# Another order of the opening's steps in a fused attention and feed-forward kernel

## The chip, the cores and the metric

The kernel runs on one core of one Trainium2 chip. The metric is the device time of one execution in microseconds (us); smaller is better.

## The reference, cut to what matters

Inputs: q, k, v of 8 batches, 8 heads, 576 tokens and 64 columns; a LayerNorm gain of 512; two weight matrices, 512 x 2048 and 2048 x 512; all float32.

```python
k_p = k.reshape(B, H, Sp, pool, D).mean(axis=3)      # pool = 8, Sp = 72
v_p = v.reshape(B, H, Sp, pool, D).mean(axis=3)
scores = scale * np.matmul(q, k_p.transpose(0, 1, 3, 2))
scores = scores - np.max(scores, axis=-1, keepdims=True)
attn = np.exp(scores)
attn = attn / (np.sum(attn, axis=-1, keepdims=True) + 1e-09)
x = np.matmul(attn, v_p)                             # heads joined: 4608 tokens x 512
xn = (x - mu) / np.sqrt(var + 1e-06) * g_ln          # over the 512 columns
out = x + np.maximum(xn @ w_ch1, 0.0) @ w_ch2
```

## The kernel before

The 4608 tokens are 36 tiles of 128, and nine chunks of four tiles. TensorE (PE) multiplies float16. Each weight and each normalized token (z) is split into a high and a low half, and a product is three matmuls (high by high, high by low, low by high).

For a token tile t, `stage_a` (A.t) loads q of tile t + 2, computes the scores (PE, L432), takes their maximum (VectorE or DVE, L441, L446), the exponentials (ScalarE or ACT, L458), splits them (ACT, and GpSimd or POOL), and sends them through a transposing DMA (L479, on SyncE's queue, SP) to give `pt`. `stage_b` (B.t) multiplies `pt` by the pooled v (PE, L537 and L538), divides by the sums (DVE, L541, L549, L551), normalizes (L562 to L632, with a chain of very short steps L619 to L621 for the inverse root), splits z (ACT L642, POOL L643) and turns it over by a transposing DMA (SP, L648). V.t is the first half of B.t, X the transposes alone.

The feed-forward part of a chunk: I.c.q is `in_quarter`, four blocks of 128 hidden columns. A block is 12 matmuls (L674) into a PSUM tile, evicted by ACT (L682) and DVE (L683) into the `ring`. O.c.h is `out_half`: for each of the chunk's four tiles 24 matmuls (L770), and one eviction on DVE (L780) that adds to x; in the second half x then goes out (SP, L784). So one O is 96 matmuls and four L780. PSUM has three tiles for these blocks, so a block can start when the third-last one before it has been evicted. The text counts the hidden blocks of chunk 0 as f0 to f15; I.0.2 holds f8 to f11, I.0.3 f12 to f15.

The kernel opens with two chunks, 0 and 1, in which it also gets the weights ready: C.m.b converts a block of matrix m, M1 and M2 take maxima for scales, S.m.b splits a block (ACT L166, DVE L171). T.h.k and U.h.k form sums of blocks of the first matrix for a product scheme of seven instead of eight partial products (DVE L277, L279, L281, POOL L278, L280; split by ACT L264 and POOL L265). HK.b.i and HV.b.i load half of a batch's k or v (SP, L299 and L312) and pool it on POOL (L304, L305, L308 for k; L318, L319, L320 for v). After a batch's last v, DVE takes its maximum (L324, then L132 and L133, with a small matmul L154) and splits it. Chunks 2 to 8 use the seven-product scheme (L705); their order is fixed by two small lists, `A_AT` and `B_AT`.

What orders the opening is the string `START`: a list of these names with their arguments. A loop calls them in that order, and so the program is recorded in that order:

```python
for token in START.split():
    name, *args = token.split(".")
    ops[name](*map(int, args))
```

The tile framework then schedules the recorded program with a timeline of its own (`schedule_with_timeline_sim=True`), so that the instructions of an engine do not stand exactly in the order of the list. Each engine runs its own instructions strictly in the order that results. After the list is through, the opening's PSUM tiles are given back, and chunks 2 to 8 follow with other PSUM pools: one for attention, and six tiles for the feed-forward part.

Of the kernel before, what the change touches and what calls it, by code (L numbers as in the profile page):

```python
# [19 lines left out]
B, H, S, D = 8, 8, 576, 64  # L20
# [34 lines left out]
Z_EXP, W1_EXP = 8, -1  # L55
OUT_EXP = -14 - W1_EXP
START = """
LD K0 A.0 C.1.0 V0 R.2.0 R.2.1 C.1.1 A.1 C.1.2 B.0 C.1.3 M1.0 S.1.0 S.1.1 S.1.2 S.1.3 R.2.2 R.2.3 B.1 A.2 I.0.0.0
A.3 B.2 I.0.1.0 LN C.2.0 B.3 C.2.1 C.2.2 C.2.3 R.1.4 R.1.5 M2.0 I.0.0.1 S.2.0 S.2.1 S.2.2 S.2.3 R.1.6 R.1.7 I.0.1.1 D.0 KN
A.4 C.1.4 C.1.5 C.1.6 VN D.1 O.0.0 C.1.7 M1.1 A.5 S.1.4 S.1.5 S.1.6 S.1.7 R.2.4 R.2.5 I.0.2 R.2.6 R.2.7 A.6 B.4 I.0.3 C.2.4 B.5 A.7 C.2.5 B.6  # L60
 C.2.6 B.7 C.2.7 M2.1  S.2.4 S.2.5 S.2.6 S.2.7 O.0.1  I.1.0 HK.2.0 HK.2.1 HV.2.0 I.1.1 HV.2.1  A.8 O.1.0
 T.1.0 T.1.1 T.0.0 T.0.1 A.9 B.8 I.1.2 HK.3.0 HK.3.1 HV.3.0 A.10 U.0.0 U.0.1 B.9 HV.3.1 A.11
V.10 I.1.3 U.1.0 U.1.1 X B.11 O.1.1
"""
RSQRT_MAGIC = float(0x5F3759DF - 0x00400000) - 2.0**31

# [841 lines left out]
```

## Time and profile before

| | before |
|---|---|
| time, median of 3 runs | 877.6 us (877.41 to 878.29) |
| time of the profiled execution | 877.42 us |
| its span in the trace | 875.7 us |
| mean granted PE clock | 0.977 |
| PE busy | 834.4 us, 95% of the span |
| DVE, ACT, POOL busy | 556.7, 324.0, 291.8 us |

The trace covers the span; the execution's own time has 1.7 us around it. Times in rows count from the span's start. A row of a timeline has start, length, engine, line, operation, output and input, the number of neighbouring instructions that it joins, and in brackets the idle time of the engine ahead of it, with what ended that. SPq is the DMA queue of SyncE. In the page's 40 slices, each digit is a busy share in tenths. The opening ends at about 279 us.

### The profile page before, as it was taken

The numbers are of one execution on the slowest core, as the hardware profiler recorded it, in microseconds if no ns is written. First come the engines' busy times: TensorE is split into PE (matmuls) and PEld (weight loads), VectorE is DVE, ScalarE is ACT, GpSimd is POOL, SyncE is SP. The second block draws the span as 40 slices with busy tenths as digits, with TensorE's granted clock in tenths as the row PEclk, the third lists the DMA queues.
The fourth block names the chain that finished last, engine by engine and source line by source line (L and its number), as shares of the span: only waits on it lengthen the run. The fifth ranks groups of instructions, "written<-read, shape, count | busy, mean of one in ns | idle before, by whom it ended". The sixth has DMA issues, their size and how long they took to land. (4 is left out here: it accounts for less than half of the span.)

```text
span 875.7 us, 14897 instructions
## 1 busy us (share of the span) xinstructions
PE 834.4 (95%) x5808; PEld 546.0 (62%) x5808; DVE 556.7 (64%) x1148; ACT 324.0 (37%) x615; POOL 291.8 (33%) x429
## 2 busy tenths in 40 slices
PE   7699896999998999999999998999999999999998
PEld 5586642454455757576767665767666676757483
DVE  4999799652376647674856486738664847494242
ACT  3797433222141524243425241524342324333140
POOL 0534687447064544245412434231111211120000
PEclk9888897999999999999999999999999999999999
DMA  9991520253154452444243415432424142322001
GB/s 354 365 385 65 127 63 7 49 134 91 37 144 122 108 113 52 121 115 120 54 124 93 98 35 137 88 76 48 126 61 71 33 115 47 51 46 64 0 1 48
DMA packets 145109, 87.35 MB, mean 100 GB/s; under 512 B 125328, under 2 KB 126480, under 8 KB 142480
## 3 DMA queue, kind: packets, MB, share of 16 engines
q1 hardware_dynamic: 143888, 85.52, 36.7%
q10 hardware_dynamic: 1152, 0.90, 0.4%
q8 instruction: 45, 0.74, 0.3%
q14 instruction: 24, 0.20, 0.1%
HBM read 45.09 MB, written 9.44 MB: 62 GB/s over the span
## 5 line engine op out<-in xcount | busy, mean ns | idle before, releaser
L770 PE MATMUL ps_f<-w,ring 128*128 128x512 f16 x1728 | 381.3, 379 | 0.0
L770 PEld LDWEIGHTS <-ring 128*128 128x128 f16 x1728 | 167.7, 98 | 193.1 <-issue 0.2
L705 PE MATMUL ps_f<-zts,w 128*128 128x256 f16 x1680 | 209.1, 274 | 7.5 <-DVE x L780 3.4
L705 PEld LDWEIGHTS <-w 128*128 128x128 f16 x1680 | 164.1, 98 | 29.7 <-issue 7.3
L780 DVE SCALAR_TENSOR_TENSOR x<-ps_f,cy,x 128x512 f32<-128x512 f32 x72 | 53.8, 748 | 120.5 <-PE ps_f L770 117.6
L674 PE MATMUL ps_f<-zts,w 128*128 128x512 f16 (+1 forms) x480 | 96.7, 363 | 10.7 <-DVE x L780 7.7
L705 PE MATMUL ps_f<-zts,tsp 128*128 128x256 f16 x672 | 96.3, 272 | 0.3 <-ACT raw L723 0.3
L746 DVE SCALAR_TENSOR_TENSOR ring<-raw,ring 128x512 f16<-128x512 f32 x112 | 83.0, 767 | 9.1 <-ACT ring L745 8.8
L469 POOL TENSOR_TENSOR phl<-e,phl 128x512 f16<-128x512 f32 x32 | 37.5, 1170 | 151.9 <-ACT phl L462 151.8
L745 ACT ACTIVATE ring<-raw 128x512 f16<-128x512 f32 x112 | 64.8, 623 | 52.4 <-DVE raw L739 52.0
L674 PEld LDWEIGHTS <-w 128*128 128x128 f16 x480 | 49.9, 105 | 51.9 <-issue 17.6
L723 ACT COPY raw<-ps_f 128x256 f32<-128x256 f32 x56 | 20.8, 372 | 140.3 <-PE ps_f L705 137.4
L705 PEld LDWEIGHTS <-tsp 128*128 128x128 f16 x672 | 64.0, 98 | 10.9 <-issue 0.7
L643 POOL TENSOR_TENSOR hl<-raw,hl 128x640 f16<-128x640 f32 x28 | 41.0, 1480 | 75.9 <-ACT hl L642 40.0
L726 DVE TENSOR_TENSOR raw<-ps_f,raw 128x256 f32<-128x256 f32 x56 | 23.7, 424 | 50.7 <-PE ps_f L705 44.6
L739 DVE TENSOR_TENSOR raw<-ps_f,raw 128x256 f32<-128x256 f32 x112 | 42.3, 418 | 21.2 <-PE ps_f L705 20.9
L318 POOL TENSOR_TENSOR vr<-vr 72x256 f32<-72x256 f32 x48 | 38.7, 813 | 47.1 <-DMA vr<-in_v_dram 46.9
L432 PE MATMUL ps_a<-kblk,q 128*128 128x144 f32 (+1 forms) x320 | 44.9, 293 | 0.0
L642 ACT CAST hl<-raw 128x640 f16<-128x640 f32 x28 | 19.2, 723 | 68.0 <-DVE raw L597 33.4
L432 PEld LDWEIGHTS ps_a<-kblk,q 128*128 128x128 f32 (+1 forms) x320 | 40.4, 183 | 5.2 <-issue 1.7
L732 DVE TENSOR_TENSOR raw<-ps_f,raw 128x256 f32<-128x256 f32 x56 | 23.6, 421 | 30.8 <-PE ps_f L705 28.0
L643 POOL TENSOR_TENSOR hl<-z,hl 128x512 f16<-128x512 f32 x18 | 21.1, 1171 | 63.0 <-ACT hl L642 47.3
(137 smaller groups left out, 991.9 us busy)
## 6 DMA issues: line engine op xcount, KB each, us to landing
q<-in_qT_dram SPq DMA_DIRECT2D x36, 256.0 KB
out_dram<-x SPq DMA_DIRECT2D x36, 256.0 KB
tsp<-in_w_dram SPq DMA_DIRECT2D x8, 1024.0 KB
kr<-in_kT_dram SPq DMA_DIRECT2D x24, 288.0 KB
vr<-in_v_dram SPq DMA_DIRECT2D x48, 144.0 KB
raw<-in_w_dram SPq DMA_DIRECT2D x6, 1024.0 KB
w<-in_kvn_dram SPq DMA_DIRECT2D x3, 1024.0 KB
ring<-in_w_dram SPq DMA_DIRECT2D x2, 1024.0 KB
```

Source lines behind the costliest of these rows:

```text
L318: eng.tensor_add(out=vr[:, 0:4, :], in0=vr[:, 0:4, :], in1=vr[:, 4:8, :])
L432: nc.tensor.matmul(ps[r, p // 2, p % 2 * 2 * KV : (p % 2 + 1) * 2 * KV], lhsT=q[:, p, r], rhs=kblk[b % NKB][:, p, :], start=True, stop=True,)
L469: nc.gpsimd.tensor_tensor(out=ph[:, 0, :, KA:P], in0=e[:, :, 0:KA], in1=ph[:, 0, :, 0:KA], op=ALU.subtract)
L643: nc.gpsimd.tensor_tensor(out=zhl[:, 1, :], in0=src, in1=zhl[:, 0, :], op=ALU.subtract)
L674: nc.tensor.matmul(ps, lhsT=w[:, part, fs], rhs=zT[:, kz, cols], start=(n == 0), stop=(n == 3 * NKT - 1),)
L705: nc.tensor.matmul(ps, lhsT=w[:, part, f * P : (f + 1) * P], rhs=z, start=start and n == 0, stop=stop and n == 3 * KH - 1, skip_group_chec ...
L726: nc.vector.tensor_tensor(out=cc[:, 0, :HC], in0=m2, in1=cc[:, 0, :HC], op=ALU.add)
L739: nc.vector.tensor_tensor(out=cc[:, j, HC:], in0=u3, in1=cc[:, j, HC:], op=ALU.add)
L745: nc.scalar.activation(out=hh[:, 0, f], in_=cc[:, j], func=AF.Relu)
L746: nc.vector.scalar_tensor_tensor(out=hh[:, 1, f], in0=cc[:, j], scalar=0.0, in1=hh[:, 0, f], op0=ALU.max, op1=ALU.subtract)
L770: nc.tensor.matmul(ps, lhsT=h[:, part, i, cols], rhs=w[:, wp, j], start=(n == 0), stop=(n == 3 * NFT // 2 - 1),)
L780: nc.vector.scalar_tensor_tensor(out=x, in0=ps, scalar=out_scale(c, tt, half), in1=x, op0=ALU.mult, op1=ALU.add)
```

## The change

The six lines of `START` are replaced by one, which holds the same tokens in another order. Nothing else is changed. All engines carry the same instructions as before.

```diff
-A.4 C.1.4 C.1.5 C.1.6 VN D.1 O.0.0 C.1.7 M1.1 A.5 S.1.4 S.1.5 S.1.6 S.1.7 R.2.4 R.2.5 I.0.2 R.2.6 R.2.7 A.6 B.4 I.0.3 C.2.4 B.5 A.7 C.2.5 B.6
- C.2.6 B.7 C.2.7 M2.1  S.2.4 S.2.5 S.2.6 S.2.7 O.0.1  I.1.0 HK.2.0 HK.2.1 HV.2.0 I.1.1 HV.2.1  A.8 O.1.0
- T.1.0 T.1.1 T.0.0 T.0.1 A.9 B.8 I.1.2 HK.3.0 HK.3.1 HV.3.0 A.10 U.0.0 U.0.1 B.9 HV.3.1 A.11
-V.10 I.1.3 U.1.0 U.1.1 X B.11 O.1.1
+... A.4 C.1.4 C.1.5 C.1.6 C.1.7 VN D.1 O.0.0 M1.1 A.5 S.1.4 S.1.5 S.1.6 S.1.7 R.2.4 R.2.5 I.0.2 R.2.6 R.2.7 A.6 B.4 C.2.6 C.2.4 B.5 A.7 C.2.5 HK.2.0 B.6 B.7 I.0.3 C.2.7 M2.1 S.2.4 S.2.5 A.8 S.2.6 S.2.7 O.0.1 I.1.0 HK.2.1 A.9 I.1.1 HV.2.0 HV.2.1 T.1.0 T.1.1 T.0.0 T.0.1 B.8 HK.3.0 O.1.0 HK.3.1 HV.3.0 A.10 U.0.0 U.0.1 B.9 I.1.2 A.11 HV.3.1 V.10 I.1.3 U.1.0 U.1.1 X B.11 O.1.1
```

The new file is five lines shorter above the functions, so a line of the changed kernel is five less than the same line before: L775 is L780, L765 is L770, L700 is L705, L427 is L432, L319 is L324, L436 is L441. The text keeps to the numbers of before.

Up to the end of O.0.0's matmuls and from the first part of chunk 2 on, the instructions stand in the same order on all engines. Between, they move. Three places matter below.

The first is DVE at the end of O.1.1. Here L780 adds the result of an output tile, and L619 to L632 are short steps of B.11's LayerNorm. Before:

```order
L620 TENSOR_TENSOR a<-a,ve 128x4
L621 SCALAR_TENSOR_TENSOR y<-a,y 128x4
L780 SCALAR_TENSOR_TENSOR x<-ps_f,cy,x 128x512
L619 TENSOR_TENSOR a<-y 128x4
...
L625 TENSOR_TENSOR y<-y,ln 128x4
L632 TENSOR_SCALAR cy<-y,c_out 128x4 x2
L780 SCALAR_TENSOR_TENSOR x<-ps_f,cy,x 128x512
L441 TENSOR_REDUCE mx<-ps_a 128x8
```

In the changed kernel the same place reads:

```order
L620 TENSOR_TENSOR y<-y,ln 128x4
L627 TENSOR_SCALAR cy<-y,c_out 128x4 x2
L775 SCALAR_TENSOR_TENSOR x<-ps_f,cy,x 128x512
L319 TENSOR_REDUCE mv<-vp 72x1
L127 TENSOR_SCALAR rowmax<-mv 72x1
L128 TENSOR_SCALAR rowmax<-rowmax 72x1
L775 SCALAR_TENSOR_TENSOR x<-ps_f,cy,x 128x512 x2
L436 TENSOR_REDUCE mx<-ps_a 128x8
```

B.11's short steps stood between the third and the fourth L780; now they are ahead of the second, and the maximum of batch 4's pooled v (L319, before L324) stands between the second and the third.

The second is PE at the same place, from the last matmul of O.1.1 to the first of chunk 2. `kblk` is the pooled k, `w_91` the first matrix. Before:

```order
L770 MATMUL ps_f<-w_92,ring 128x512
L432 MATMUL ps_a<-kblk_113,q 128x144 x4
L705 LDWEIGHTS w_91
L705 MATMUL ps_f<-zts,w_91 128x256
```

Now:

```order
L765 MATMUL ps_f<-w_92,ring 128x512
L427 MATMUL ps_a<-kblk_113,q 64x144
L427 MATMUL ps_a<-kblk_114,q 64x144
...
L700 LDWEIGHTS w_91
L700 MATMUL ps_f<-zts,w_91 128x256
```

The scores of A.12 (128 rows) stood between; they have moved ahead of O.1.1. The scores of A.13 (64 rows of two batches), which stood inside chunk 2's first products, have taken their place. B.11's values moved from after 45 of O.1.1's 96 matmuls to after 11, and B.10's from inside O.1.1 to the end of I.1.2.

The third is DVE around O.1.0. Before:

```order
L441 TENSOR_REDUCE mx<-ps_a 128x8
L324 TENSOR_REDUCE mv<-vp 72x1
L683 SCALAR_TENSOR_TENSOR ring<-ps_f,ring 128x512
L446 TENSOR_TENSOR e<-ps_a,mx 128x576
L132 TENSOR_SCALAR rowmax<-mv 72x1
L133 TENSOR_SCALAR rowmax<-rowmax 72x1
L780 SCALAR_TENSOR_TENSOR x<-ps_f,cy,x 128x512 x4
L541 TENSOR_SCALAR sm<-ps_a,cv 128x8
```

Now:

```order
L775 SCALAR_TENSOR_TENSOR x<-ps_f,cy,x 128x512 x3
L319 TENSOR_REDUCE mv<-vp 72x1
L127 TENSOR_SCALAR rowmax<-mv 72x1
L128 TENSOR_SCALAR rowmax<-rowmax 72x1
L775 SCALAR_TENSOR_TENSOR x<-ps_f,cy,x 128x512
L436 TENSOR_REDUCE mx<-ps_a 128x8
```

The maximum of batch 3's pooled v stood ahead of O.1.0's first L780, and now stands between the third and the fourth; behind it comes the maximum of A.10's scores.

Elsewhere: on PE the values of B.5 to B.7 and the scores of A.8 now come ahead of O.0.1 (B.6 and B.7 lay inside it, A.8 behind it). On DVE one L277 passes O.0.0's second L780, and in I.0.3 the eviction of f12 (L683) stands behind one more L281 and part of B.5's LayerNorm. On ACT an L264 each comes ahead of the evictions L682 of f9 to f12. On POOL the L643 of B.5 to B.7 and the k sums of batch 3 come earlier, the v sums of batch 3 later. On SP the transposes, loads and stores follow their steps.

More of the change, by code (lines that the diff above doesn't have):

```diff
@@ L57 @@
 START = """
-LD K0 A.0 C.1.0 V0 R.2.0 R.2.1 C.1.1 A.1 C.1.2 B.0 C.1.3 M1.0 S.1.0 S.1.1 S.1.2 S.1.3 R.2.2 R.2.3 B.1 A.2 I.0.0.0
-A.3 B.2 I.0.1.0 LN C.2.0 B.3 C.2.1 C.2.2 C.2.3 R.1.4 R.1.5 M2.0 I.0.0.1 S.2.0 S.2.1 S.2.2 S.2.3 R.1.6 R.1.7 I.0.1.1 D.0 KN
-A.4 C.1.4 C.1.5 C.1.6 VN D.1 O.0.0 C.1.7 M1.1 A.5 S.1.4 S.1.5 S.1.6 S.1.7 R.2.4 R.2.5 I.0.2 R.2.6 R.2.7 A.6 B.4 I.0.3 C.2.4 B.5 A.7 C.2.5 B.6
- C.2.6 B.7 C.2.7 M2.1  S.2.4 S.2.5 S.2.6 S.2.7 O.0.1  I.1.0 HK.2.0 HK.2.1 HV.2.0 I.1.1 HV.2.1  A.8 O.1.0
- T.1.0 T.1.1 T.0.0 T.0.1 A.9 B.8 I.1.2 HK.3.0 HK.3.1 HV.3.0 A.10 U.0.0 U.0.1 B.9 HV.3.1 A.11
-V.10 I.1.3 U.1.0 U.1.1 X B.11 O.1.1
+LD K0 A.0 C.1.0 V0 R.2.0 R.2.1 C.1.1 A.1 C.1.2 B.0 C.1.3 M1.0 S.1.0 S.1.1 S.1.2 S.1.3 R.2.2 R.2.3 B.1 A.2 I.0.0.0 A.3 B.2 LN C.2.0 I.0.1.0 B.3 C.2.1 C.2.2 R.1.4 C.2.3 M2.0 R.1.5 I.0.0.1 S.2.0 S.2.1 S.2.2 S.2.3 R.1.6 R.1.7 I.0.1.1 D.0 KN A.4 C.1.4 C.1.5 C.1.6 C.1.7 VN D.1 O.0.0 M1.1 A.5 S.1.4 S.1.5 S.1.6 S.1.7 R.2.4 R.2.5 I.0.2 R.2.6 R.2.7 A.6 B.4 C.2.6 C.2.4 B.5 A.7 C.2.5 HK.2.0 B.6 B.7 I.0.3 C.2.7 M2.1 S.2.4 S.2.5 A.8 S.2.6 S.2.7 O.0.1 I.1.0 HK.2.1 A.9 I.1.1 HV.2.0 HV.2.1 T.1.0 T.1.1 T.0.0 T.0.1 B.8 HK.3.0 O.1.0 HK.3.1 HV.3.0 A.10 U.0.0 U.0.1 B.9 I.1.2 A.11 HV.3.1 V.10 I.1.3 U.1.0 U.1.1 X B.11 O.1.1
 """
```

## The prediction

> **What bounds the kernel now.** I read the page first: which engine is busiest, and where in the 40 slices it isn't.
>
> ```profile
> PE 834.4 (95%) x5808; PEld 546.0 (62%) x5808; DVE 556.7 (64%) x1148; ACT 324.0 (37%) x615; POOL 291.8 (33%) x429
> ...
> PE   7699896999998999999999998999999999999998
> ```
>
> PE is busy for 834.4 of 875.7 us. Its holes lie in the first seven slices of 21.9 us (to about 153 us) and at the end. The same matmuls are issued after the change, so only PE's idle stretches, and stretches in which its clock is reduced, can be won or lost. The instructions of all engines are in the same order up to about 126 us, and again from the first part of chunk 2 (about 285 us). So I asked for PE's waits between 100 and 300 us, and then for those behind.
>
> ```profile
> PE ps_f L674 <- DVE x L780: 7.7, 2, 4.2
> PE ps_f L705 <- DVE x L780: 3.0, 1, 3.0
> PE ps_f L674 <- DVE ring L683: 1.2, 1, 1.2
> ```
>
> ```profile
> PE ps_f L705 <- DVE raw L726: 1.5, 1, 1.5
> ```
>
> That second row is the largest wait from 300 us on. From there PE is the bound, so a shift at 285 us is still there at the end. Four waits lie in the changed stretch: 7.7, 3.0 and 1.2 us. PE's timeline places them (start, length, then the idle time before).
>
> ```profile
> 135.67 4.38 PE L674 MATMUL ps_f<-zts,w 128*128 128x512 f16 x12 [4.25 <-DVE x L780]
> ...
> 143.60 5.28 PE L674 MATMUL ps_f<-zts,w 128*128 128x512 f16 x12 [3.49 <-DVE x L780]
> ...
> 161.00 2.75 PE L674 MATMUL ps_f<-zts,w 128*128 128x512 f16 x12 [1.16 <-DVE ring L683]
> ```
>
> ```profile
> 265.76 9.01 PE L770 MATMUL ps_f<-w,ring 128*128 128x512 f16 x41
> 274.61 1.14 PE L432 MATMUL ps_a<-kblk,q 128*128 128x144 f32 x8
> 278.78 5.10 PE L705 MATMUL ps_f<-zts,w 128*128 128x256 f16 x30 [3.02 <-DVE x L780]
> ...
> 286.43 0.70 PE L432 MATMUL ps_a<-kblk,q 128*64 128x144 f32 x6
> ```
>
> ```profile
> 292.41 0.95 PE L432 MATMUL ps_a<-kblk,q 128*64 128x144 f32 x10
> ```
>
> ```profile
> 324.90 3.44 PE L705 MATMUL ps_f<-zts,w 128*128 128x256 f16 x30
> ```
>
> The wait at 278.78 costs more than its 3.02 us. The 30 matmuls behind it took 5.10 us; 30 of the same kind took 3.44 us at 324.90. The granted clock (the column after POOL's busy time) says why:
>
> ```profile
> 278.00:280.00 2.00, 1.22 (x7) 0.90 (x7) 1.97 (x4) 0.00 (x0) 0.00 (x0) 0.74 0.88 225
> 280.00:282.00 2.00, 2.00 (x11) 1.35 (x10) 0.18 (x1) 0.96 (x2) 0.00 (x0) 0.50 0.62 193
> ```
>
> It was 0.50 from 280 to 282 us. [...]
>
> What held that L780, the fourth of O.1.1? DVE's timeline, then POOL's:
>
> ```profile
> 271.73 0.15 DVE L620 TENSOR_TENSOR a<-a,ve 128x4 f32<-128x4 f32 x1
> ...
> 272.85 3.84 DVE L620 TENSOR_TENSOR a<-a,ve 128x4 f32<-128x4 f32 x1
> ...
> 277.98 0.74 DVE L780 SCALAR_TENSOR_TENSOR x<-ps_f,cy,x 128x512 f32<-128x512 f32 x1
> ```
>
> ```profile
> 272.82 0.72 POOL L318 TENSOR_TENSOR vr<-vr 72x256 f32<-72x256 f32 x1 [1.37 <-DMA vr<-in_v_dram]
> 273.50 1.40 POOL L643 TENSOR_TENSOR hl<-raw,hl 128x640 f16<-128x640 f32 x1
> 274.86 0.45 POOL L319 TENSOR_TENSOR vr<-vr 72x128 f32<-72x128 f32 x1
> 275.27 1.39 POOL L643 TENSOR_TENSOR hl<-raw,hl 128x640 f16<-128x640 f32 x1
> ```
>
> One L620 on four columns took 0.15 us and the next 3.84. That one began and ended with an unbroken run of POOL (272.82 to 276.66), two of whose four pieces split B.11's z. Behind it stand the rest of B.11's small steps, and only then the L780 whose operands PE had finished by 274.77.
>
> **The change, term by term.** *End of O.1.1 (the gain).* B.11 moves from after 45 of O.1.1's 96 products to after 11. In before it stood at 263.08; a whole half of products, O.1.0, took 20.88:
>
> ```profile
> 208.37 20.88 PE L770 MATMUL ps_f<-w,ring 128*128 128x512 f16 x96
> ...
> 263.08 0.19 PE L537 MATMUL ps_a<-va,pt 128*128 128x65 f16 x1
> ```
>
> 34 products of 0.2175 us (20.88 / 96) are 7.4 us, so its LayerNorm, its small steps and POOL's two L643 come about 6 to 7 us earlier, and the third and fourth L780 stand side by side behind them.
>
> The fourth L780 then waits for PE alone: 0.74 us from the last product. A.13's scores (16 records, 0.70 + 0.95 us in the rows at 286.43 and 292.41, which overlap their neighbours a little) now stand on PE between O.1.1 and L705, so that time is covered; A.12's, which filled it before, went ahead of O.1.1. PE does the same scores, elsewhere. Terms: −3.02 for the wait and −1.66 (5.10 − 3.44) for the half clock behind it. Bounds: zero if another wait of 3 us stands there (rivals), −4.9 if the fourth L780's own 0.2 us behind its operands is covered too. I take −4.68. Chunk 2's z transposes follow B.11 on SP and come earlier too; nothing of that is on the path.
>
> *The two waits of about 4 us in I.0.2.* They are the rows at 135.67 and 143.60, and end with O.0.0's third and fourth L780. In the new order the same DVE instructions stand ahead of each of these. One L277 has passed ahead of the second L780, which holds an earlier block of I.0.2; the 4.25 us wait right behind hides that. An L277 is short there:
>
> ```profile
> 134.27 0.68 DVE L277 TENSOR_TENSOR raw<-w 128x512 f32<-128x512 f16 x1
> ```
>
> Both waits stay: 0. Bounds: one L277, 0.68 us, either way.
>
> *I.0.3 and O.0.1.* B.5, B.6, B.7 and A.8 go ahead of O.0.1 on PE; before, B.6 and B.7 lay inside it and A.8 behind it.
>
> ```profile
> 163.82 6.21 PE L770 MATMUL ps_f<-w,ring 128*128 128x512 f16 x28
> ```
>
> ```profile
> 186.67 7.93 PE L674 MATMUL ps_f<-zts,w 128*128 128x512 f16 x36
> ```
>
> O.0.1 starts at 163.82 and I.1.0 at 186.67, without a wait on PE between; the scores and values that change places there only exchange PE time. Two DVE rows bear on the rest:
>
> ```profile
> 157.44 1.63 DVE L281 TENSOR_TENSOR raw<-raw 128x512 f32<-128x512 f32 x1 [0.78 <-POOL raw L280]
> ```
>
> ```profile
> 268.74 0.55 DVE L572 TENSOR_SCALAR raw<-x,ln 128x512 f32<-128x512 f32 x1
> ```
>
> What may change is the 1.16 us wait at 161.00: f12's L683 (the eviction whose buffer f15 needs) now stands behind one L281, already 1.63 us long before, and behind a part of B.5's LayerNorm (its L572 alone takes 0.55), while the first blocks of I.0.3 start no earlier. PE has B.6 and part of A.8 to do meanwhile. By these durations f15 would start near 161.7, not 161.0, with 1.0 us of A.8 and B.6 already behind it: −0.3 net. Between −1.2 (wait gone) and +2.7 (rival 3) I take 0, nearest to that balance.
>
> *Batch 3's pooled v.* Its loads (SP, L312), its sums (POOL, L318 to L320) and its maximum (DVE, L324) come later: HV.3.0 now follows O.1.0 in the list. L324 stands between the third and fourth L780 of O.1.0 (before: ahead of the first). Behind it: the fourth L780, A.10's maximum L441, its exponentials, its transposed p (SP, L479), and B.10 on PE. Its POOL chain ran before from
>
> ```profile
> 189.16 0.59 POOL L320 TENSOR_TENSOR vp<-vr 72x64 f32<-72x64 f32 x2 [0.73 <-DVE cvm L522]
> ```
>
> to
>
> ```profile
> 212.72 0.32 POOL L320 TENSOR_TENSOR vp<-vr 72x64 f32<-72x64 f32 x1
> ```
>
> 23.9 us, with the sums of K's halves and other POOL work among it; HK.2.1 and part of HK.3 now come ahead of it. It can start about 210 us, when batch 2's v is split; I take three quarters of 23.9, 18 us, and so L324 at 228. O.1.0, still some 21 us from 208.7, ends near 229.6, so L324 is in time for the fourth L780, and has until 231 before A.10's p is late (rival 2). Cost 0; bounds 0 and +7.3. SP's p of A.7 (L479) no longer waits for B.5's end near 164, and ACT's L682 in I.0.3 stand behind one L264 more each; both are in the estimate for f15.
>
> *Sum.* 877.42 − 3.02 − 1.66 = 872.74, say 872.7. The profiled execution (877.42 us, span 875.7 and 1.7 around it) stands 0.2 under the median, 877.6; that is inside the rounding. The forecast's own range is 871.8 to 874.8: −0.9 for the I.0.3 wait and overlap, +2 for half of the clock term and small new waits.
>
> **Rivals.** A difference of 0.2% (1.75 us) is about what a measurement can tell from none.
>
> 1. *A wait takes the place of the one removed* (877.4, chance 0.13). Batch 4's maximum L324 now stands between the second and third L780 of O.1.1. Before it stood at
>
> ```profile
> 267.86 0.68 DVE L324 TENSOR_REDUCE mv<-vp 72x1 f32<-72x512 f32 x1 [1.61 <-POOL vp L320]
> ```
>
> and had waited for POOL. If its POOL chain, which now has B.11's two L643 (2.8 us) in front, ends after about 275.5, DVE holds both last L780 for it, and PE waits 3 us and gets the half clock again. For it: that 1.61. Against: with 2.8 us more it is due at 271, 4.5 us ahead of the need.
>
> 2. *Slower: batch 3's maximum comes too late* (about 880.0, chance 0.11). Four rows price it: what may stand in front, and the way from an L441 to the transposed p.
>
> ```profile
> 233.58 1.16 POOL L643 TENSOR_TENSOR hl<-z,hl 128x512 f16<-128x512 f32 x1 [15.21 <-ACT hl L642]
> ```
>
> ```profile
> 234.77 1.23 SPq L648 DMA_TRANSPOSE zts<-hl  x1
> ```
>
> ```profile
> 241.15 0.76 DVE L441 TENSOR_REDUCE mx<-ps_a 128x8 f32<-128x576 f32 x1 [2.25 <-PE ps_a L432]
> ```
>
> ```profile
> 248.25 2.43 SPq L479 DMA_TRANSPOSE pt<-phl  x1
> ```
>
> If its POOL chain still needs 23.9 us, and POOL and SP put a z's L643 and transposes in front (1.16 + 1.23), L324 starts at 210.1 + 23.9 + 2.4 = 236.4, A.10's L441 follows at about 238. From an L441 to the p on its way took 9.5 us in before (241.15 to 250.68). So p is there at 248, and B.10, due on PE near 242.4 (before, it came inside O.1.1), waits 5.6 us, and pays 1.7 of half clock: +7.3 − 4.7 = 2.6 slower. It decides from a chain of 20.7 us on; at 23.9 alone the wait is 3.2 and the gain is just eaten; from 25.5 the kernel is slower by 0.2%. For it: in before DVE stood idle 3.74 us on this very chain:
>
> ```profile
> 213.07 0.68 DVE L324 TENSOR_REDUCE mv<-vp 72x1 f32<-72x512 f32 x1 [3.74 <-POOL vp L320]
> ```
>
> Against: the K halves, which shared POOL with it, come earlier.
>
> 3. *DVE is held in I.0.3* (875.4, chance 0.10). POOL runs without a break from 157.37 to 161.20:
>
> ```profile
> 157.37 3.83 POOL L265 TENSOR_TENSOR w<-raw,w 128x512 f16<-128x512 f32 x3
> ```
>
> If L281 or L572, now ahead of f12's L683, is held as L620 was (3.84 for 0.15), f12's buffer comes free near 162 and f15 starts 2.7 us later. [...] Against: L281 at 157.44 took 1.63 in the same run of POOL and wasn't held to its end.
>
> 4. *More* (870.5, 0.04): the 1.16 us wait goes too, and one of the 4 us waits shrinks by one L277.
>
> **From here to the numbers.** Forecast 0.62, rivals 0.13, 0.11, 0.10, 0.04. The range 871.4 to 877.7 holds the forecast, rival 3 and rival 1; it leaves out rival 2 and the far gain, and a little of the tails. Faster by over 0.2% (under 875.85): 0.62 + 0.04 + most of rival 3 = 0.74. Within it: 0.13 + 0.02 = 0.15. Slower: 0.11.
>
> **What would show it.** Right: no L705 wait on L780 of 3 us at the start of chunk 2, a clock of 1.00 there, L620 at 0.15 us near 272, A.13's scores ahead of L705, the two waits near 135 and 143 still about 4 us. Wrong: an L537 of B.10 with a wait on pt near 242; L324 with POOL as releaser ahead of the last L780 of O.1.0 or O.1.1; a longer wait at f15; or a shift at 285 us that PE loses again before the end.

## The result and the profile after

The changed kernel took 871.45 us (median of 4 runs, 870.89 to 872.24) against 877.5 us (4 runs, 876.09 to 878.29). The ratio is 0.9933, with a 95% interval of 0.9916 to 0.9951: faster by 0.5 to 0.8%. Beside the experiments it was measured again, 872.67 against 878.16 us, ratio 0.9936 (0.9913 to 0.9959). The prediction was 872.7 us. The profiled execution took 870.89 us, its span is 868.8. One of the twelve executions of the kernel with the filler, below, ran at a granted clock of 0.582 and took 1398.31 us; it is left out of every comparison.

PE's waits between 100 and 300 us, after:

```profile
PE ps_f L669 <- DVE x L775: 6.6, 2, 3.5
PE ps_f L669 <- DVE ring L678: 1.0, 2, 0.5
```

The wait of L700 (L705 before) on the fourth L775 (L780) is gone. PE's timeline at the places of the prediction, after:

```profile
134.10 4.44 PE L669 MATMUL ps_f<-zts,w 128*128 128x512 f16 x12 [3.17 <-DVE x L775]
...
142.03 5.28 PE L669 MATMUL ps_f<-zts,w 128*128 128x512 f16 x12 [3.46 <-DVE x L775]
```

```profile
274.16 1.20 PE L427 MATMUL ps_a<-kblk,q 128*64 128x144 f32 x16
275.29 3.45 PE L700 MATMUL ps_f<-zts,w 128*128 128x256 f16 x30
```

A.13's scores lie between O.1.1 and L700, no idle time stands in brackets, and the 30 matmuls take 3.45 us, not 5.10. The granted clock there (column after POOL's busy time):

```profile
276.00:280.00 4.00, 4.00 (x40) 3.57 (x37) 1.38 (x3) 3.45 (x8) 0.46 (x2) 1.00 0.68 201
```

DVE and POOL at the end of O.1.1, after:

```profile
263.77 1.39 DVE L615 TENSOR_TENSOR a<-a,ve 128x4 f32<-128x4 f32 x1
265.19 1.32 DVE L616 SCALAR_TENSOR_TENSOR y<-a,y 128x4 f32<-128x4 f32 x1
...
268.87 0.74 DVE L775 SCALAR_TENSOR_TENSOR x<-ps_f,cy,x 128x512 f32<-128x512 f32 x1
269.92 0.68 DVE L319 TENSOR_REDUCE mv<-vp 72x1 f32<-72x512 f32 x1 [0.32 <-POOL vp L315]
...
274.27 0.75 DVE L775 SCALAR_TENSOR_TENSOR x<-ps_f,cy,x 128x512 f32<-128x512 f32 x1 [2.64 <-PE ps_f L765]
```

```profile
263.74 2.75 POOL L638 TENSOR_TENSOR hl<-raw,hl 128x640 f16<-128x640 f32 x2 [1.16 <-ACT hl L637]
```

The short steps are still held (two of them for 1.39 and 1.32 us, beside POOL's two L638), but now about nine microseconds earlier (L607, the first of their chain, starts at 260.25 us instead of 269.20). The last L775 waits for PE, not PE for it.

The two spans differ by 6.9 us. Where they part, by the starts of rows; the first is O.0.0, before and after:

```profile
107.95 20.88 PE L770 MATMUL ps_f<-w,ring 128*128 128x512 f16 x96
```

```profile
107.46 20.88 PE L765 MATMUL ps_f<-w,ring 128*128 128x512 f16 x96
...
185.11 7.93 PE L669 MATMUL ps_f<-zts,w 128*128 128x512 f16 x36
```

| stretch on PE | before | after | difference |
|---|---|---|---|
| start to O.0.0 (same order in both) | 107.95 | 107.46 | −0.49 |
| O.0.0 to the end of the first wait in I.0.2 | 27.72 | 26.64 | −1.08 |
| from there to I.1.0 | 51.00 | 51.01 | 0.0 |
| I.1.0 to the end of O.1.1 and A.12 | 89.09 | 89.05 | 0.0 |
| from there to the end of the first 30 matmuls of chunk 2 | 8.12 | 4.58 | −3.54, with A.13's 1.13 us now in it |
| the rest | 591.82 | 590.06 | −1.76, of which A.13's 1.13 |

So 4.7 us come from the end of the opening (3.54 + 1.13, with A.13's scores counted as moved), 1.1 from the first wait in I.0.2, 0.6 from the rest, and 0.5 from ahead of the change. Where the 0.6 lie isn't shown: PE's waits from 300 us on add up to 4.7 us before and 4.6 after.

### The profile page after: what moved, and what is told of

It reads as the page before. It is cut to its first block, busy times and chain, and to the rows that moved or that the text cites. A ratio compares the mean times of both kernels' runs of the same rounds, so it can differ in the third digit from the quotient of the medians.

```text
span 868.8 us, 14907 instructions
## 1 busy us (share of the span) xinstructions
PE 831.3 (96%) x5808; PEld 545.2 (63%) x5808; DVE 561.1 (65%) x1148; ACT 324.3 (37%) x615; POOL 294.9 (34%) x429
## 5 line engine op out<-in xcount | busy, mean ns | idle before, releaser
L765 PE MATMUL ps_f<-w,ring 128*128 128x512 f16 x1728 | 380.7, 379 | 0.0
L765 PEld LDWEIGHTS <-ring 128*128 128x128 f16 x1728 | 167.8, 98 | 193.9 <-issue 0.2
L700 PE MATMUL ps_f<-zts,w 128*128 128x256 f16 x1680 | 207.1, 273 | 3.2 <-DVE raw L721 1.5
L700 PEld LDWEIGHTS <-w 128*128 128x128 f16 x1680 | 163.3, 98 | 23.9 <-issue 2.8
L775 DVE SCALAR_TENSOR_TENSOR x<-ps_f,cy,x 128x512 f32<-128x512 f32 x72 | 53.8, 748 | 124.7 <-PE ps_f L765 122.4
L700 PE MATMUL ps_f<-zts,tsp 128*128 128x256 f16 x672 | 96.1, 272 | 1.5 <-DVE rowmax L127 1.2
L700 PEld LDWEIGHTS <-tsp 128*128 128x128 f16 x672 | 64.0, 98 | 12.1 <-issue 1.9
L638 POOL TENSOR_TENSOR hl<-raw,hl 128x640 f16<-128x640 f32 x28 | 41.0, 1479 | 78.9 <-ACT hl L637 43.0
L453 ACT ACTIVATE e<-e 128x576 f32<-128x576 f32 x32 | 21.8, 683 | 62.6 <-DVE e L441 44.5
L427 PE MATMUL ps_a<-kblk,q 128*128 128x144 f32 (+1 forms) x320 | 44.7, 292 | 0.0
L427 PEld LDWEIGHTS ps_a<-kblk,q 128*128 128x128 f32 (+1 forms) x320 | 40.5, 183 | 5.7 <-issue 2.0
```

Of the source, the lines that this page charges most:

```text
L427: nc.tensor.matmul(ps[r, p // 2, p % 2 * 2 * KV : (p % 2 + 1) * 2 * KV], lhsT=q[:, p, r], rhs=kblk[b % NKB][:, p, :], start=True, stop=True,)
L638: nc.gpsimd.tensor_tensor(out=zhl[:, 1, :], in0=src, in1=zhl[:, 0, :], op=ALU.subtract)
L700: nc.tensor.matmul(ps, lhsT=w[:, part, f * P : (f + 1) * P], rhs=z, start=start and n == 0, stop=stop and n == 3 * KH - 1, skip_group_chec ...
L765: nc.tensor.matmul(ps, lhsT=h[:, part, i, cols], rhs=w[:, wp, j], start=(n == 0), stop=(n == 3 * NFT // 2 - 1),)
L775: nc.vector.scalar_tensor_tensor(out=x, in0=ps, scalar=out_scale(c, tt, half), in1=x, op0=ALU.mult, op1=ALU.add)
```

## Experiments

Experiments that were measured together share runs of the kernel before on the same chip: 876.99 us for the first four, 878.16 for the run with L643 on DVE, the changed kernel again and the first two on I.0.2, 876.37 for the last two. Executions scatter by some us from the start on: O.0.0 (PE, L770) began at 104.00 us in one trace here (the run with L643 on DVE) and at 112.30 in another (the end alone), with the same instructions in the same order ahead of it. So the traces are compared from O.0.0 on, or at one place. All line numbers below are those of before. The code is cut to the lines that matter, with one statement to a line.

**The end alone.** One name of the list of before is moved:

```diff
-T.0.1 A.9 B.8 I.1.2 HK.3.0 HK.3.1 HV.3.0 A.10 U.0.0 U.0.1 B.9 HV.3.1 A.11
+T.0.1 A.9 B.8 HK.3.0 HK.3.1 HV.3.0 A.10 U.0.0 U.0.1 B.9 I.1.2 HV.3.1 A.11
```

> The list of before with one name moved: I.1.2 goes behind B.9. On PE that gives the end of the opening nearly as in the changed kernel (A.12 ahead of O.1.1, B.11 after 14 of its 96 matmuls, A.13 between O.1.1 and L705), and leaves I.0.2, I.0.3 and O.0.1 as before. Theory (the gain is the wait of 3.0 us on O.1.1's fourth L780 and 1.7 us of half clock behind it): no such wait, clock 1.00, about 872.8 us; the two waits of about 4 us stay. Rival (the gain comes from I.0.2 to O.0.1, where the measured kernel was 1.6 us ahead by 134 us): 876 to 877.5.

874.84 against 876.99 us, ratio 0.9972 (0.9951 to 0.9992): faster, by less than the 4.7 us. PE's timeline in its trace, at the last waits of the opening and in chunk 4:

```profile
264.54 1.76 PE L770 MATMUL ps_f<-w,ring 128*128 128x512 f16 x6 [1.02 <-ACT ring L682]
```

```profile
282.26 3.45 PE L705 MATMUL ps_f<-zts,w 128*128 128x256 f16 x30
```

```profile
423.36 1.44 PE L705 MATMUL ps_f<-zts,w 128*128 128x256 f16 x6 [2.93 <-DVE rowmax L132]
```

The wait at L705 is gone and the 30 matmuls take 3.45 us, as the theory has it. But a wait of 1.02 us stands inside O.1.1, on an eviction of ACT, and one of 2.93 us in chunk 4, where before had 0.54. So wait and half clock, 4.7 us, go at their place, and in this trace the order gives much of it back elsewhere. This trace is of the slowest of the twelve executions (881.24 us), so it isn't shown that the others have these two waits too. By the times, the end alone is worth 2.5 us (0.7 to 4.3), and the theory's 872.8 was missed.

**The middle alone.** The new list up to O.0.1, the old one behind it:

```diff
-A.6 B.4 I.0.3 C.2.4 B.5 A.7 C.2.5 B.6 C.2.6 B.7 C.2.7 M2.1 S.2.4 S.2.5 S.2.6 S.2.7 O.0.1 I.1.0 HK.2.0 HK.2.1 HV.2.0 I.1.1 HV.2.1 A.8 O.1.0
+A.6 B.4 C.2.6 C.2.4 B.5 A.7 C.2.5 HK.2.0 B.6 B.7 I.0.3 C.2.7 M2.1 S.2.4 S.2.5 A.8 S.2.6 S.2.7 O.0.1 I.1.0 HK.2.1 HV.2.0 I.1.1 HV.2.1 O.1.0
```

> The middle of the new list (up to O.0.1) with the rest of the old one: on all engines I.0.2, I.0.3 and O.0.1 stand as in the changed kernel, with one L277 ahead of O.0.0's second L780, and the end of O.1.1 stands as before. Theory: the wait of 3.0 us and the half clock at L705 stay; only the first wait in I.0.2 may be shorter, by about 1.1 us as in the changed kernel's trace: 876.4, or 877.5 if that was chance. Rival (the middle brings the gain): 871 to 873.

875.87 us, ratio 0.9985 (0.9966 to 1.0003). Its trace:

```profile
137.55 4.44 PE L674 MATMUL ps_f<-zts,w 128*128 128x512 f16 x12 [2.78 <-DVE x L780]
```

```profile
280.72 5.10 PE L705 MATMUL ps_f<-zts,w 128*128 128x256 f16 x30 [2.95 <-DVE x L780]
```

```profile
282.00:284.00 2.00, 2.00 (x11) 1.40 (x10) 0.38 (x2) 0.81 (x2) 0.00 (x0) 0.50 0.57 169
```

The wait and the half clock at L705 are both there again. By the times the middle brings 1.3 us, with an interval from 3.0 us faster to 0.3 slower; the rival's 871 to 873 falls.

**Filling the wait.** Before, with matmuls that do nothing needed, placed by the scheduler between O.1.1 and A.12 (`filler[0]` is a block of the `ring` that O.1.1 has just read):

```diff
+    ps = psum["ps_m"].tile([P, CH], F32, name="ps_m")
+    for i in range(12):
+        nc.tensor.matmul(ps, lhsT=wt[2][:, 0, 0, 0:P], rhs=filler[0], start=(i == 0), stop=(i == 11))
     first.close()
```

> Before, with 12 matmuls of 512 columns added on PE between O.1.1 and A.12's scores, into a PSUM tile that nothing reads: they fill about 2.6 of the 3.0 us that PE waits for the fourth L780. Theory (the wait's end is set by DVE, and the half clock follows from PE standing idle): L705 starts at the same time, its first 30 matmuls take 3.4 instead of 5.1 us, 875.8 us in all. [...] If the filler delays the path: over 878.

877.51 us against 876.99, ratio 1.0004 (0.9986 to 1.0022). Its trace at L705, and at a later place beside the same place of before:

```profile
279.15 3.45 PE L705 MATMUL ps_f<-zts,w 128*128 128x256 f16 x30
```

```profile
540.00:546.00 6.00, 4.17 (x34) 3.37 (x33) 3.39 (x7) 1.83 (x3) 0.79 (x3) 0.94 0.26 87
546.00:560.00 14.00, 14.00 (x129) 12.21 (x128) 8.82 (x19) 8.96 (x23) 2.82 (x4) 0.90 0.26 57
```

```profile
541.00:547.00 6.00, 4.16 (x37) 3.46 (x35) 3.39 (x7) 1.74 (x3) 0.84 (x3) 1.00 0.27 87
547.00:561.00 14.00, 13.68 (x135) 11.99 (x133) 9.91 (x22) 9.55 (x24) 2.85 (x4) 1.00 0.29 63
```

At its place the theory holds: with PE kept busy, the 30 matmuls take 3.45 instead of 5.10 us. The 1.7 us do not show in the times, though: 877.51 us, where the theory has 875.8. In this trace two things ran against it: the first wait in I.0.2 was 5.64 us, and the clock was reduced once more at 540 to 560 us, where before's was full. That the other executions had the same isn't shown. So the half clock behind the wait is shown as a local cost, and its share of the total isn't.

**The short steps behind the last L780.** Before, with one tiny DVE step that ties the short steps to O.1.1's last output tile, x of tile 7 (`last` collects the x tiles in the order of their L780):

```diff
+        if c == 2:
+            nc.vector.tensor_scalar_mul(out=ve, in0=last[-2][:, 0:TPC], scalar1=0.0)
         nc.vector.tensor_scalar(
```

> Before, with the chain of short DVE steps (L607 to L632, the scales for chunk 2's outputs) made to depend on O.1.1's last output tile, by one tiny added DVE step; so the fourth L780 stands right behind the third, and PE's order is that of before, B.11 late. Theory (the L780 was late because it stood behind short steps that POOL's run held up): L780 runs at about 275 us, PE waits under 0.5 us, clock 1.00: about 872.8. Rival (B.11's earlier place is what counts, or POOL's run holds the L780 itself): the wait stays at 2 to 3 us, 876 to 877.5.

874.12 us against 876.99, ratio 0.9971 (0.9953 to 0.9989). DVE, POOL and PE in its trace:

```profile
274.02 0.75 DVE L780 SCALAR_TENSOR_TENSOR x<-ps_f,cy,x 128x512 f32<-128x512 f32 x1 [3.10 <-PE ps_f L770]
```

```profile
272.18 1.39 POOL L643 TENSOR_TENSOR hl<-raw,hl 128x640 f16<-128x640 f32 x1
273.54 0.45 POOL L319 TENSOR_TENSOR vr<-vr 72x128 f32<-72x128 f32 x1
273.95 1.40 POOL L643 TENSOR_TENSOR hl<-raw,hl 128x640 f16<-128x640 f32 x1
```

```profile
276.65 2.90 PE L705 MATMUL ps_f<-zts,w 128*128 128x256 f16 x24 [1.01 <-DMA zts<-hl]
```

With B.11 as late as before, the fourth L780 waits for PE alone, though POOL runs beside it, and the wait of 3.0 us is gone. So it was these steps' place in DVE's order that held it. A second wait, 1.01 us on the transposed z of B.11, comes to light behind the first six matmuls; the theory had less than 0.5 us. In the changed kernel, with B.11 earlier, it is not there. By the times this edit is worth 2.5 us (1.0 to 4.1); the theory's 872.8 was missed, and 1.0 of the difference is this wait.

**POOL's part.** Before, with the low halves of B.11's z (L643) on DVE:

```diff
-        nc.gpsimd.tensor_tensor(out=zhl[:, 1, :], in0=src, in1=zhl[:, 0, :], op=ALU.subtract)
+        (nc.vector if max(X) == 11 and n == 5 else nc.gpsimd).tensor_tensor(out=zhl[:, 1, :], in0=src, in1=zhl[:, 0, :], op=ALU.subtract)
```

> Before, with the two L643 of B.11 on DVE instead of POOL; DVE carries them between L619 and the L620 that took 3.84 us, nothing else moves on DVE. Theory (that L620 was held by POOL's unbroken run): it takes about 0.15 us, the two L643 about 0.8 each, the fourth L780 comes 1 to 2 us earlier, and PE's wait falls from 3.0 to 1 to 2 us. Rival (L620 waited for something else): it still takes over 2 us, and the wait grows to 4 us or more.

One run, 871.2 us against 878.16; 4 us of that lie ahead of O.0.0 (104.00 against 107.95), so only the place counts here. DVE and PE:

```profile
269.38 2.08 DVE L643 TENSOR_TENSOR hl<-raw,hl 128x640 f16<-128x640 f32 x2
271.39 0.41 DVE L620 TENSOR_TENSOR a<-a,ve 128x4 f32<-128x4 f32 x1
```

```profile
273.88 3.44 PE L705 MATMUL ps_f<-zts,w 128*128 128x256 f16 x30 [1.22 <-DVE x L780]
```

L620 takes 0.41 us in place of 3.84, the wait is 1.22 in place of 3.02, and behind it the clock stays full (1.00 from 274 to 278 us): the 30 matmuls take 3.44 us. Together with the 1.39 and 1.32 us beside POOL's two L638 after, this shows POOL's run as the reason of the 3.84.

**The changed kernel again.**

> The changed kernel itself, beside the kernel before on the same chip as the experiments. Theory: no wait at L705 in chunk 2, 16 scores of A.13 ahead of it, first wait in I.0.2 between 3.2 and 4.3 us (what that wait does from run to run is the question: the first trace had 3.17). Time 871.4 to 872.8 against 877.

The times are given above. No wait at L705, A.13 ahead of it, and the first wait in I.0.2:

```profile
135.44 4.44 PE L674 MATMUL ps_f<-zts,w 128*128 128x512 f16 x12 [3.10 <-DVE x L780]
```

3.17 and 3.10 us in the two traces of this kernel, and 2.78 + 0.73 in the middle-only kernel, which has the same order there; 4.25, 5.64, 4.26 and 5.12 in four traces with the order of before, but 3.47 in the fifth (the end alone).

**The waits of I.0.2.** Four kernels on top of the changed one. The first ties the weight sums T to an output tile (`last[3]` and `X[3]` are O.0.0's fourth), the second the four splits S.2.4 to S.2.7 too:

```diff
+            nc.vector.tensor_scalar_mul(out=t_raw["b"][:, :, 0:1], in0=last[3][:, 0:4].unsqueeze(2), scalar1=0.0)
...
+        h and nc.vector.tensor_scalar_mul(out=ws[:, 1:2], in0=X[3][:, 0:1], scalar1=0.0)
         nc.vector.tensor_mul(out=ws[:, h : h + 1], in0=f1[:, h : h + 1], in1=s)
```

> The changed kernel with the weight sums T (DVE L277, L279, L281, POOL L278, L280, L265) made to depend on O.0.0's fourth output tile, by one tiny DVE step: they run after O.0.1 starts, and ahead of O.0.0's second to fourth L780 stand only the four weight splits L171, a few short steps and batch 2's maximum. Theory (the two waits of 3 to 4 us in I.0.2, and the half clock around them, come from DVE work that could run later, made longer by POOL's runs beside it): second wait gone, first wait 0 to 2 us, 864 to 867 us. Rival (the splits alone, or the p of B.5 to B.7, set the time there): waits move behind I.0.2, 870 to 872.

> As the run with the sums late, and the four splits L171 of the second matrix's other half (needed by O.0.1) also made to depend on O.0.0's fourth output tile: its four L780 then stand next to each other. Theory: both waits of I.0.2 gone (6.6 us) and its 24 matmuls at full clock (4.44 + 5.28 against 2 x 2.75 us): up to 10.8 us below the changed kernel, 861 to 864. Rival (the splits come too late for O.0.1, or the transposed p of A.6 and A.7 for B.6 and B.7): a new wait of 3 us or more ahead of O.0.1, 866 to 871.

870.02 us, ratio 0.9905 (0.9886 to 0.9924), and 869.66 us, 0.9894 (0.9873 to 0.9916). PE's waits between 108 and 300 us in the kernel with the sums late:

```profile
PE ps_f L674 <- DVE ring L683: 5.3, 3, 2.1
PE ps_f L770 <- DVE vh L392: 3.4, 1, 3.4
```

The waits of I.0.2 are gone, but 10 us of others came later, from I.1.1 to I.1.2, among the sums (these two rows, and waits of 0.8 and 0.6 us). In the second kernel it is some 7 us at the same places. Both theories were missed: the waits moved behind I.0.2, as the first rival says, though not to the place that the second names. T stands behind O.0.1 in the list, and O.0.1 writes the same tile once more; so the sums came behind O.0.1, not behind O.0.0 as the expectation says. The place was wrong, so T was moved ahead of O.0.1 in the list:

```diff
-S.2.6 S.2.7 O.0.1 I.1.0 HK.2.1 A.9 I.1.1 HV.2.0 HV.2.1 T.1.0 T.1.1 T.0.0 T.0.1 B.8
+S.2.6 S.2.7 T.1.0 T.1.1 T.0.0 T.0.1 O.0.1 I.1.0 HK.2.1 A.9 I.1.1 HV.2.0 HV.2.1 B.8
```

> The changed kernel with the sums T named ahead of O.0.1 in the list and made to depend on O.0.0's fourth output tile (in the runs with the sums late, T stood behind O.0.1 in the list, so that the tile they waited for was the one O.0.1 writes). The sums then run between O.0.0's last L780 and O.0.1's first, among the evictions of I.0.2 and I.0.3; from O.0.1's first L780 on, DVE and PE stand as in the changed kernel. Theory (the waits of I.0.2 are the sums and splits ahead of two L780, and what the late sums lost again was their place beside batch 2's v): no wait on L780 over 1.5 us, evictions L683 in I.0.2 and I.0.3 a little late behind sums of up to 2.5 us each, no wait at O.1.0: 865 to 869. Rival (the sums cost the same wherever they stand while the same POOL runs lie beside them): waits of 3 us in all and more on L683, 870 to 873.

864.35 us, ratio 0.9865 (0.9845 to 0.9884): the best version here, 12 us below before and a little under the theory's 865; the changed kernel's 0.9936 is 6 us above it by the ratios. DVE around O.0.0's last two L780, PE's waits from 108 to 300 us, and the clock:

```profile
130.38 1.40 DVE L780 SCALAR_TENSOR_TENSOR x<-ps_f,cy,x 128x512 f32<-128x512 f32 x2
```

```profile
PE ps_f L674 <- DVE ring L683: 2.2, 2, 1.2
PE ps_f L674 <- DVE x L780: 1.5, 1, 1.5
PE ps_a L537 <- DVE x L551: 1.2, 1, 1.2
```

```profile
120.00:140.00 20.00, 20.00 (x97) 9.14 (x96) 14.71 (x20) 5.78 (x7) 11.32 (x14) 1.00 0.15 36
140.00:160.00 20.00, 16.47 (x116) 8.43 (x115) 18.98 (x28) 7.92 (x14) 17.98 (x14) 1.00 0.25 55
```

Waits of 4.9 us instead of 7.6, and a full clock in I.0.2, where the changed kernel has 0.91 and 0.83 in the same two windows. From O.0.0 to I.1.0 PE takes 70.65 us (109.86 to 180.51) instead of the changed kernel's 77.65 (107.46 to 185.11). So the two waits of I.0.2 and the half clock behind them did come from the sums' place on DVE, and the rival falls. Last, with the splits tied down as well:

> As the run with the sums in the middle, and the four splits L171 of the second matrix also behind O.0.0's fourth output tile. Theory: no wait on L780 in I.0.2 at all; the splits and the sums share the time to O.0.1, so some sums end inside O.0.1 and its L780 come late; 865 to 870. Rival: too much DVE work ahead of O.0.1, waits on L683 and L780 of 5 us and more, 871 to 875.

881.89 us, ratio 1.007 (1.0047 to 1.0093), slower than before. PE waits where I.1.0 starts:

```profile
191.89 1.44 PE L674 MATMUL ps_f<-zts,w 128*128 128x512 f16 x3 [12.91 <-DVE rs L549]
```

```profile
173.40 4.77 DVE L277 TENSOR_TENSOR raw<-w 128x512 f32<-128x512 f16 x1
```

```profile
189.06 1.31 SPq L648 DMA_TRANSPOSE zts<-hl  x1
```

I.1.0 needs the z of B.7. Its values were done on PE inside O.0.1, at about 164 us, but on DVE its steps take turns with the last sums, one of which took 4.77 us: its z was written from 183.69 us on, and the transposing DMA started at 189.06. (The trace names L549, the last on DVE, but that belongs to B.8; L674 reads `zts`, the transposed z.) The rival was right about the sign; its place and its 871 to 875 were not what came.

## Why the prediction was right

*The end of O.1.1* (−4.68 predicted): −4.67 measured (3.02 for the wait, and 5.10 − 3.45 for the 30 matmuls). Both halves hold at their place: the end alone removes wait and half clock, the middle alone keeps both (2.95 us, 5.10 us), the filler removes the half clock alone. The reason given also holds: short steps in DVE's order (run with the scales late), held by POOL (run with L643 on DVE). One sign did not come as named, an L620 of 0.15 us near 272: in the changed kernel one of the chain took 1.39 us at 263.77, too early to hold an awaited L780. One thing is open: as changes of the time, the end alone (2.5 us) and the middle alone (1.3) add up to 3.8 us, and the changed kernel has 5.6 to 5.9 by the ratios; the intervals allow that, and no run shows where the rest comes from. One name was loose: the steps L619 to L632 are not B.11's own normalization but the scales for chunk 2's outputs, which need B.11's statistics and are not needed before those outputs.

*The first wait in I.0.2* (0, bounds 0.68 us either way): −1.08. This is the term that was mis-sized. The DVE instructions ahead of the third L780 are indeed the same, but how long they take differs with what POOL does beside them (an L277 took 2.51 us beside POOL's work and 0.68 while POOL stood idle), and the prediction took their number, not their time. Before, DVE's steps behind the second L780:

```profile
126.73 2.51 DVE L277 TENSOR_TENSOR raw<-w 128x512 f32<-128x512 f16 x1
129.16 2.69 DVE L171 SCALAR_TENSOR_TENSOR w<-w,ws 128x1024 f16<-128x1024 f32 x1
131.78 0.80 DVE L277 TENSOR_TENSOR raw<-w 128x512 f32<-128x512 f16 x1
133.07 1.28 DVE L171 SCALAR_TENSOR_TENSOR w<-w,ws 128x1024 f16<-128x1024 f32 x1 [0.49 <-ACT w L166]
```

After, the same steps; the first of them is the one that has passed ahead of the second L780:

```profile
125.44 1.64 DVE L272 TENSOR_TENSOR raw<-w 128x512 f32<-128x512 f16 x1
127.01 0.74 DVE L775 SCALAR_TENSOR_TENSOR x<-ps_f,cy,x 128x512 f32<-128x512 f32 x1
127.67 1.51 DVE L166 SCALAR_TENSOR_TENSOR w<-w,ws 128x1024 f16<-128x1024 f32 x1
129.10 2.17 DVE L272 TENSOR_TENSOR raw<-w 128x512 f32<-128x512 f16 x1
131.19 1.47 DVE L166 SCALAR_TENSOR_TENSOR w<-w,ws 128x1024 f16<-128x1024 f32 x1
```

One more L277 follows in each, of 0.68 us before and 0.80 after. The first two steps became 2.1 us shorter, the other three 1.7 us longer; that is 0.4 us net, and the stop of 0.49 us on ACT's half of the split is gone. Before, POOL stood idle from 132.03 to 136.29 us, and there an L277 took 0.68 and a split 1.28 us; ahead of that, beside POOL's work, they took 2.51 and 2.69. Over all traces the waits are 3.5 to 5.6 us in the order of before and 3.1 to 3.5 in the new one; the ranges touch, so the direction is likely and the 1.1 us not settled, and which POOL step held which was not tried. The second wait stayed (3.46 against 3.49). That both waits could be removed, the run with the sums in the middle shows.

*I.0.3 and O.0.1* (0): 0.0 by the table. The wait of 1.16 us at f15 became 0.52 + 0.48 at f12 and f13 (1.69 + 0.47 in the second trace); f15 itself did not wait. So the sum came out as taken, but not by the forecast's way, a later f15.

*Batch 3's pooled v* (0): its maximum ran at 227.20, forecast 228:

```profile
227.20 0.68 DVE L319 TENSOR_REDUCE mv<-vp 72x1 f32<-72x512 f32 x1 [3.34 <-POOL vp L315]
...
228.29 0.75 DVE L775 SCALAR_TENSOR_TENSOR x<-ps_f,cy,x 128x512 f32<-128x512 f32 x1
```

Its fourth L775 followed at once, and B.10 did not wait, so rival 2 fell. Rival 1 fell by the row at 269.92: batch 4's maximum came 4.4 us ahead of the last L775. Both rows are what the prediction names as a sign of being wrong, a maximum with POOL as releaser ahead of the last L780: DVE did stand idle for POOL there, 3.34 and 0.32 us, but PE did not wait for it. The sign was too strict. Rival 3 fell too: no step of I.0.3 was held long enough to make f15 wait.

What the sum left out are small changes behind the opening (−0.6) and the scatter ahead of it (−0.5). With the first wait's −1.1 they bring the profiled execution 1.8 us below the forecast. The median of the first measurement, 871.45, lies under the forecast's own range (871.8 to 874.8) and just inside the wider one, which begins at 871.4; that it stayed inside is luck. In the second measurement the gain was 5.5 us, and the forecast's 4.7 lies in both intervals (4.3 to 7.4 and 3.6 to 7.6 us).

## What to carry to other kernels

When an engine that is not the bound holds the bound one, look at which of its instructions stand ahead of the awaited one in its queue and whether they are needed yet: here steps wanted much later held an eviction, and one tiny dependency moved them. Price such steps by their time beside the other engines' work, not by their count: here one L620 took 0.15 us, and the next, beside POOL's run, 3.84. An idle stretch of the bound engine can cost more than its length (here 3.02 us of wait and 1.66 us behind it at a granted clock of 0.50), so check the clock behind it. And moving work later only helps if its new place has room: against the changed kernel, and by the ratios to before, the same sums gained 3 us behind O.0.1 and 6 ahead of it, and with the splits added 12 were lost.

## What the runs showed of the hardware

A stall of 3.02 us on PE (before) and one of 2.95 us (the middle alone) were each followed by some 2 us at a granted clock of 0.50; behind stalls of 1.22 us (L643 on DVE) and 1.01 us (the scales late) 30 of L705's matmuls took 3.44 and 24 took 2.90 us, close to their pace without a stall (30 in 3.44 us in before at 324.90, 24 in 2.78 us in the filler's trace at 554.79). But the length of a stall does not settle it. At the same place of O.1.0, first with the sums late, then with the splits late too:

```profile
208.51 15.28 PE L770 MATMUL ps_f<-w,ring 128*128 128x512 f16 x70 [3.44 <-DVE vh L392]
```

```profile
205.77 16.97 PE L770 MATMUL ps_f<-w,ring 128*128 128x512 f16 x70 [2.71 <-DVE vh L392]
```

At 0.2175 us each, 70 of these matmuls take 15.2 us. So behind the stall of 3.44 us they kept that pace, 15.28 us, and behind the one of 2.71 us they took 1.7 us more. Near 543 us, stalls of 0.31 and 1.52 us within 2 us went with a clock of 0.94 and then 0.90 in the filler's trace, and stalls of 0.33 and 1.52 us with 1.00 in that of before. So about the same idle time went with a reduced clock in one execution and with a full one in another. What decides between the two is not shown.

One DVE step on 128 x 4 elements (an L620; the one before it took 0.15 us) was held for 3.84 us, through four POOL instructions that followed each other without a gap (272.82 to 276.66 us); that is longer than any one of the four (1.40 at most). In the changed kernel two such steps took 1.39 and 1.32 us and ended at 265.16 and 266.51 us, within 0.1 us of the ends of POOL's two L638 (1.40 us each, from 263.74 and 265.10). With POOL's two L643 moved to DVE, the step took 0.41 us.
